# Strassen's seven products in place of eight for two projection banks of the first eight token tiles

## The chip, the cores and the metric

The kernel runs on one core of a Trainium2 chip. The metric is the device time of one execution in microseconds (us), the median of several runs. The engines are named as in the profile: PE is the matrix engine (TensorE), PEld its weight load, DVE the vector engine, ACT the scalar engine, POOL the GpSimd engine, and SP the engine whose queue issues the DMA transfers. A "bank" is one of the eight PSUM banks, 128 rows by 512 float32 columns.

## The reference, cut to what matters

The block adds to its input x (2048 tokens of 640 features) a linear attention over the normalised x and an MLP over the twice normalised x.

```python
xn = _layernorm(x)
q, k, v = split(xn @ wqkv)                   # 32 heads of 20
pq, pk = q @ w_phi, k @ w_phi                # per head
phi = concat([softmax(p), softmax(-p)])      # for pq and for pk
kv, z = phi_k^T @ v, sum(phi_k)              # per head
o = (phi_q @ kv) / (phi_q @ z + 1e-6)
out = x + o @ wo + gelu(layernorm(xn) @ w1 + b1) @ w2 + b2
```

Softmax over 20 features needs a maximum, a minimum, two differences, an exponential and a sum for k and for q of each token.

## The kernel before, in words

All large products are done in float32 exactly split into two parts, "hi" and "lo" (`split`: ACT writes hi as a rounded copy, DVE or POOL writes lo as the difference). A product of two split matrices takes three matmuls: hi by hi, hi by lo, lo by hi.

The work stands in stages that follow each other on PE. First come the MLP passes of the first 1024 tokens (`Mlp.passes(g, b, ...)`, g from 0 to 6 for hidden chunks and b 0 or 1 for 512 tokens each); beside them the other engines prepare: `prep` folds w_phi into wk and wq (tiles wkh and wkl, 128 rows by 5 chunks of the contraction by their columns) and writes the normalised tokens 1024 to 2047 to DRAM. From there to about 430 us stand the projections of 16 token tiles of 128 tokens. The rest of the span holds the MLP of the second 1024 tokens, the attention and the output projection. In the MLP of the second half and in the output projection the kernel before already uses Strassen's scheme.

A projection tile t has four banks, in the order i = 0, 1, 2, 3: columns 0 to 511 (features of k), 512 to 1023 (the rest of k, then features of q), 320 columns (the rest of q, a part of v), and 512 columns of v. `proj(t, i)` issues the 15 matmuls of one bank, 5 chunks by 3, into one of three rotating banks (`ptile`, banks 0 to 2). `evacuate` copies a bank with ACT into one of four buffers `pks` (two in tile m3, two in m4): 0 for k, 1 + t % 3 for q. `features` takes maximum and minimum on DVE (L932, L933), two differences on POOL (L938), the exponential on ACT (L939) and the sum on DVE (L941), in one of three buffers e (m0, m1, m2 in turn). `k_tile` divides on POOL (L949) and splits the result into the one buffer ft (tile w1, L60 and L63); `q_tile` divides on POOL (L992, L995) and transposes on DVE (L1001). `v_parts` splits v out of the bank (ACT L965, DVE L967). `kv_tile(t - 2)` multiplies ft by v into the five banks 3 to 7 (L974), and once into a rotating bank (L978) that DVE adds to kxa. The split of wo (L60, L63, five of them) stands beside tiles 1, 2, 3, 6 and 7.

On PE everything is in the order in which it is written. DVE, ACT and POOL are in written order up to the end of the MLP passes (`order.close()`) and again late in the span; in the projections a list scheduler sets their order when the program is built, so that each of these engines has one fixed queue. A tile with one buffer is given out again when its last reader is done.

Of the kernel before, what the change touches and what calls it, by code (L numbers as in the profile page):

```python
# [15 lines left out]
P = 128  # L16
# [34 lines left out]
def tile_kernel(ctx: ExitStack, tc: tile.TileContext, x, xT, wkT, wqT, wv, wphi, wo, w1, b1, w2, b2,  # L51
# [42 lines left out]
    a_dram = [tc.dram_tile([P, KC, 512], F32, name=f"a{b}") for b in range(2)]  # L94
    d_dram = [[tc.dram_tile([H, 512], F32, name=f"d{i}{b}") for i in range(2)] for b in range(NB)]
# [555 lines left out]

    jobs = [units[o:o + 2] for o in range(0, 14, 2)]
# [54 lines left out]
    wkv_ = [kvw.tile([P, KC, CN], F32R, name=f"wk{p}") for p in "hl"]  # L707
    def prep_fold(batch, ts, done=None):
# [26 lines left out]
    def more_stats():  # L735

        def tiles():
            xbs = {}
            for t in (*range(8, 16), None):
                if t is not None:  # L740
                    xbs[t] = fp.tile([P, 2, KC, G5], F32, name="t").rearrange("p a c f -> p (a c f)")[:, :D]
# [4 lines left out]
        yield from stats(range(8, 16), fp, tiles())  # L746
        for _ in range(2):
            yield
        yield from rows(2, 2, fp, mlp.px, 5)

    def prep():
# [18 lines left out]
        split(*[w[:, :, C2:C3] for w in wkv_], raw)  # L770

        xs, hls, events = {}, {}, []

        def load(c, b):
            xs[c, b] = fp.tile([P, 512], F32, name="xq", bufs=4)
# [9 lines left out]
        def hi(*at):  # L785
            hls[at] = fp.tile([P, 2, KC, G5], F32R, name="t").rearrange("p a c f -> p a (c f)")[:, :, :512]
# [23 lines left out]

        base = 8
# [18 lines left out]

    def load_v():

        raws = [fp.tile([P, 2, KC, G5], F32, name="t").rearrange("p a c f -> p (a c f)") for _ in range(2)]
        raws = [raw[:, o:o + VF * H] for raw in raws for o in (0, VF * H)] + [fp.tile([P, D], F32, name="raw")[:, :VF * H]]
# [9 lines left out]

    p01 = mlp.passes(0, 1, [wc[0], wc[1]])
    next(p01)
    mlp.beside = prep()
# [9 lines left out]
    for g in range(2, 7):  # L857
        for b in range(2):
# [4 lines left out]
            if (g, b) == (6, 1):  # L863
                mlp.beside = split_v()
# [13 lines left out]
    rs.close()  # L878
    order.close()
    for b in range(2):  # L880
# [6 lines left out]
    acc[2] = ctx.enter_context(tc.tile_pool(name="acc2", bufs=1)).tile([P, KC, 512], F32, name="acc2")  # L887
# [14 lines left out]
    def proj(t, i):  # L902
# [4 lines left out]
        ps = ptile()[:, :wh.shape[2]]  # L907
# [19 lines left out]
    def features(t, n):  # L927

        turn[0] += 1
        p3 = pks[0 if n == "k" else 1 + t % 3].rearrange("p (h f) -> p h f", f=DH)  # L930
# [13 lines left out]
    def k_tile(t):  # L944
        e, sm = features(t, "k")
# [6 lines left out]
        split(fh, fl, e)  # L952
# [17 lines left out]
    def kv_tile(t, ft, v):  # L970
# [6 lines left out]
        ps = ptile()[:, :160]  # L977
# [7 lines left out]
    def q_tile(t):  # L985


        e, sm = features(t, "q")
# [9 lines left out]
        if i == 0:  # L998
            ets[b] = [places[n % 5] for n in range(4 * b, 4 * b + 4)]
# [9 lines left out]
    fts, ets = {}, {}  # L1009
    TAIL = [(14, 0), (14, 1), (15, 0), (15, 1), (14, 2), (14, 3), (15, 2), (15, 3)]  # L1010
    places = [acc01.tile([P, KC, 512], F32, name=f"acc{n}").rearrange("p c (j n) -> p (c j) n", n=P) for n in range(2)]
    places = [p[:, j:j + 10] for p in places for j in (0, 10)] + [et.tile([P, 10, P], F32, name="et")]


    for t, i in [(t, i) for t in range(14) for i in range(4)] + TAIL:
        if (t, i) in ((4, 0), (8, 0)):
            b = t // 4 + 1
            y[b] = [yp.tile([P, KC, 512], F32R, name=f"y{p}{b % 2}") for p in range(2)]
            for p in range(2):
                nc.sync.dma_start(f(y[b][p]), y_dram[b - 2][p])  # L1020
        ps = proj(t, i)
        pq = 1 + t % 3
        if t and t % 4 == 0:
# [7 lines left out]
        elif i == 2:  # L1031
            evacuate(ps[:, C3 - C2:], pq, B1F)
            v_parts(t, ps, VF)
            q_tile(t)
# [636 lines left out]
```

## Time and profile before

| what | value |
|---|---|
| median of 3 runs | 700.89 us (700.73 to 700.99) |
| the profiled execution | 701.24 us |
| its span | 699.5 us |
| PE busy | 693.6 us, 99% of the span |
| DVE, ACT, POOL busy | 523.3, 365.2, 437.9 us |
| projections of 16 tiles | from about 211 to 430 us |
| granted clock of PE | 1.0 |

The span is the time from the first to the last recorded instruction; the rest of the execution lies around it. Busy time of an engine is the union of its instructions. A group of instructions is given with its count, its busy time and the mean time of one; for PE that mean is the latency of one matmul, and the time from one start to the next is shorter, since matmuls overlap.

### The profile page before, as it was taken

How to read it: one execution, taken by the hardware profiler on the slowest of the kernel's cores; microseconds unless marked ns; L12 is line 12 of the kernel's file. 1: busy time of each engine (PE TensorE's matmuls, PEld its weight loads, DVE VectorE, ACT ScalarE, POOL GpSimd, SP SyncE). 2: the span in 40 equal slices, each digit the busy share in tenths (PEclk: the TensorE clock that was granted, in tenths of full speed). 3: DMA queues.
4: the chain of work that ended last, by engine and by line, in shares of the span. 5: the costliest groups of instructions: out<-in, count | busy, mean ns of one | idle time of the engine just before them, and what ended most of it. 6: DMA issues, size and time to landing. Idle time of an engine off the chain costs nothing.

```text
span 699.5 us, 9720 instructions
## 1 busy us (share of the span) xinstructions
PE 693.6 (99%) x3331; PEld 584.8 (84%) x3331; DVE 523.3 (75%) x859; ACT 365.2 (52%) x617; POOL 437.9 (63%) x324
## 2 busy tenths in 40 slices
PE   8999999999999999999999999999999999999998
PEld 7888888888888888888888888888888888888886
DVE  7778654987754787788878888948688686789783
ACT  6434643344433545554544546557676666659350
POOL 3711314566245886687666869648689997577930
PEclk9999999999999999999999999999999999999999
DMA  9834633485634227326500705874355548881222
GB/s 315 256 126 124 198 109 99 158 268 172 210 116 155 81 90 227 93 75 205 136 1 1 189 0 201 284 210 128 111 149 160 184 148 291 287 278 63 76 76 105
DMA packets 67463, 107.61 MB, mean 154 GB/s; under 512 B 7622, under 2 KB 31974, under 8 KB 65790
## 3 DMA queue, kind: packets, MB, share of 16 engines
q1 hardware_dynamic: 67110, 106.98, 48.1%
q8 instruction: 26, 0.43, 0.3%
q14 instruction: 23, 0.19, 0.1%
q10 hardware_dynamic: 304, 0.01, 0.0%
HBM read 72.42 MB, written 34.55 MB: 153 GB/s over the span
## 4 chain that ended last, share of the span: by engine, by line
PE 96%; DVE 2%; DMA 0%; issue 0%; ACT 0%; DVEq 0%
PE bank L913 29%; PE bank L69 19%; PE bank L70 19%; PE bank L71 19%; PE bank L974 3%; PE bank L648 2%; PE bank L1208 1%; PE bank L1209 1%; PE bank L554 1%; PE bank L313 1%; PE bank L332 1%; PE bank L312 1%; PE bank L331 1%; DVE st L137 0%; DMA xb<-in_x 0%; DVE rx L1257 0%
## 5 line engine op out<-in xcount | busy, mean ns | idle before, releaser
L913 PE MATMUL bank<-wkh,y 128*128 128x512 f32 (+1 forms) x480 | 139.8, 365 | 0.0
L69 PE MATMUL bank<-m,w 128*128 128x512 f32 x288 | 113.1, 393 | 0.0
L70 PE MATMUL bank<-m,w 128*128 128x512 f32 x288 | 112.2, 390 | 0.0
L63 POOL TENSOR_TENSOR w<-r,w 128x640 fp32r<-128x640 f32 x32 | 52.6, 1656 | 92.8 <-ACT w L60 62.3
L71 PE MATMUL bank<-m,w 128*128 128x512 f32 x266 | 103.7, 390 | 0.0
L69 PE MATMUL bank<-y,w 128*128 128x512 f32 (+1 forms) x256 | 99.7, 389 | 0.0
L70 PE MATMUL bank<-y,w 128*128 128x512 f32 (+1 forms) x256 | 99.0, 387 | 0.0
L913 PEld LDWEIGHTS bank<-wkh,y 128*128 128x128 f32 x480 | 87.5, 188 | 12.9
L71 PE MATMUL bank<-y,w 128*128 128x512 f32 (+1 forms) x246 | 95.1, 387 | 0.0
L913 PE MATMUL bank<-wkl,y 128*128 128x512 f32 (+1 forms) x240 | 87.1, 363 | 0.0
L69 PEld LDWEIGHTS bank<-m,w 128*128 128x128 f32 x288 | 54.1, 188 | 11.4 <-issue 0.4
L70 PEld LDWEIGHTS bank<-m,w 128*128 128x128 f32 x288 | 54.1, 188 | 10.9
L938 POOL TENSOR_TENSOR m<-m,mx 128x640 f32<-128x640 f32 x32 | 42.1, 1315 | 31.9 <-DVE mx L932 31.8
L939 ACT ACTIVATE m<-m,rs_all 128x1280 f32<-128x1280 f32 x32 | 43.7, 1364 | 30.4 <-POOL m L938 30.4
L71 PEld LDWEIGHTS bank<-m,w 128*128 128x128 f32 x266 | 49.9, 188 | 10.4
L941 DVE TENSOR_REDUCE sm<-m 128x64 f32<-128x1280 f32 x32 | 47.3, 1477 | 13.9 <-ACT m L939 13.7
L336 DVE TENSOR_TENSOR acc<-bank,acc 128x512 f32<-128x512 f32 x70 | 47.3, 684 | 13.6 <-PE bank L71 8.4
L913 PE MATMUL bank<-w,y 128*128 128x512 f32 x240 | 57.4, 391 | 0.0
L69 PEld LDWEIGHTS bank<-y,w 128*128 128x128 f32 x256 | 48.1, 188 | 10.4 <-ACT bank L1276 0.3
L70 PEld LDWEIGHTS bank<-y,w 128*128 128x128 f32 x256 | 48.1, 188 | 9.4
L71 PEld LDWEIGHTS bank<-y,w 128*128 128x128 f32 x246 | 46.2, 188 | 9.4
L949 POOL TENSOR_TENSOR m<-m,w 128x1280 f32<-128x1280 f32 x16 | 39.2, 2448 | 20.4 <-DVE w L947 18.4
(242 smaller groups left out, 1524.7 us busy)
## 6 DMA issues: line engine op xcount, KB each, us to landing
r<-in_w SPq DMA_DIRECT2D x52, 320.0 KB
e<-e SPq DMA_DIRECT2D x40, 256.0 KB
e<-acc SPq DMA_DIRECT2D x52, 160.0 KB
t<-t SPq DMA_DIRECT2D x8, 512.0 KB
acc<-in_xT SPq DMA_DIRECT2D x3, 1280.0 KB
tf<-t SPq DMA_DIRECT2D x2, 1536.0 KB
xb<-in_x SPq DMA_DIRECT2D x8, 320.0 KB
t<-in_x SPq DMA_DIRECT2D x8, 320.0 KB
```

The lines of the kernel that those rows point to most:

```text
L63: eng.tensor_tensor(lo, src, f(hi), op=ALU.subtract)
L69: nc.tensor.matmul(ps, lh, rh, start=first, stop=False, **kw)
L70: nc.tensor.matmul(ps, lh, rl, start=False, stop=False, **kw)
L71: nc.tensor.matmul(ps, ll, rh, start=False, stop=last, **kw)
L336: nc.vector.tensor_tensor(acc[b][:, m, :], pw, acc[b][:, m, :], op=ALU.add)
L648: nc.tensor.matmul(ps[:, u * nh * DF:(u + 1) * nh * DF], raw[:nh * DH, u * P:(u + 1) * P], wpt[:nh * DH, g, :nh, 1:], start=True, stop=True)
L913: nc.tensor.matmul(ps, lh[:, kc, c], rh[:, kc], start=n == 0, stop=n == 3 * KC - 1)
L938: subs[n, t] = nc.gpsimd.tensor_tensor(ep[:, :, s], a, b, op=ALU.subtract)
L939: exps[n, t] = nc.scalar.activation(e, e, AF.Exp, scale=rs_all[:, t:t + 1])
L941: nc.vector.tensor_reduce(sm, e.rearrange("p a (h f) -> p (a h) f", f=DH), axis=AX, op=ALU.add)
L949: nc.gpsimd.tensor_tensor(e3, e3, w.unsqueeze(2).to_broadcast([P, 2 * H, DH]), op=ALU.mult)
L974: nc.tensor.matmul(kvp[g // 2][:, (g % 2) * 240:(g % 2) * 240 + 240].rearrange("p (i c) -> p i c", i=2), v[:, g * VS:(g + 1) * VS], ft[:, ...
```

## The change

For tokens 0 to 1023 the tiles are taken in pairs, (0, 1) to (6, 7), and banks 0 and 1 of a pair are computed together. Of the five contraction chunks, 0 and 1, and 2 and 3, form two 2x2 block products (token tile by chunk, times chunk by bank). Each takes seven block products in Strassen's form (Winograd's variant) in place of eight; chunk 4 (`rest`) is done as before.

- On the side of the weights four sums of blocks, s1 to s4, are needed for each pair of chunks q. `raw_sums` builds them (four adds on DVE, four on POOL for each q), `split_sums` splits them (ACT and DVE). For q = 0 the raw sums stand in the events of `prep`, their splits in `sums_end` beside the last two MLP passes (g = 6), where the raw sums for q = 1 stand too; the splits for q = 1 follow the MLP (`late`). s3 replaces the block a21 in wkh and wkl, which is stored to DRAM before (`open_sums`) and loaded back after the last pair.
- On the side of the tokens four differences t1 to t4 are built on POOL beside the MLP passes (`turned_forms`: for each of two 512-token blocks and each q, 2 adds of 512 columns and 4 subtractions of 256), split on ACT and DVE and stored to DRAM in 16 transfers; `load_forms` loads 1 MB of them before each pair into the one buffer w0.
- On PE a pair has 7 x 2 x 3 + 4 x 3 = 54 matmuls for the two banks, where the two tiles had 2 x 2 x 15 = 60. `sevens` sets their order: bank 0 holds product a11 b11, to which s2 t2 and then s3 t3 and a rest are added, and each time a partial sum is complete it is copied out (ACT) before PE goes on in that bank; bank 1 holds s1 t1, to which s4 b22 is added; bank 2 holds two products that are only added. So of the four results of a pair each is an ACT copy (`move`, L1174) and then a DVE add (L1172) into `pks`.
- `pks` 0 and 1 are now k of the two tiles, 2 and 3 their q. The lo part of k features is half on DVE and half on POOL. PE's order in the first pair is: bank i = 2 of both tiles (`narrow`), i = 3 of both (`wide`), then `sevens`; the next pair's `sevens` follow at once. In later pairs: `sevens` (with `kv_tile(t - 2)` in it), two `narrow`, `wide(0, 2)`, `kv_tile(t - 1)`, `wide(1, 2)`; both `wide` use bank 2.
- The splits of wo stand beside tiles 8, 9 and 10.

Tiles 8 to 15 are computed as before. The core of the diff:

```diff
-    def proj(t, i):
+    def proj(t, i, ps=None):
...
-        ps = ptile()[:, :wh.shape[2]]
+        ps = (ps or ptile())[:, :wh.shape[2]]
...
-        p3 = pks[0 if n == "k" else 1 + t % 3].rearrange("p (h f) -> p h f", f=DH)
+        p3 = pks[i].rearrange("p (h f) -> p h f", f=DH)
...
-        split(fh, fl, e)
+        if t < 8:
+            nc.scalar.activation(fh, e, AF.Copy)
+            for s, eng in enumerate((nc.vector, nc.gpsimd)):
+                eng.tensor_tensor(fl[:, s], e[:, s], f(fh[:, s]), op=ALU.subtract)
+        else:
+            split(fh, fl, e)
...
+    def pair(t, yt, start):
...
+        def product(ps, w, yn, first=False, last=False):
+            for q in range(2):
+                for n, (pl, pr) in enumerate(((0, 0), (0, 1), (1, 0))):
+                    nc.tensor.matmul(ps, left(yn, pl, q), right(w, pr, q), start=first and q == 0 and n == 0,
...
+        def move(ps, i, j, add):
+
+            parts = [(ps, j, 1)] if i == 0 else [(ps[:, :KQ - 512], j, 1 + 512 // H), (ps[:, KQ - 512:], 2 + j, 1)]
...
+                if add:
+                    nc.vector.tensor_tensor(o, src, o, op=ALU.add)
+                else:
+                    nc.scalar.activation(o, src, AF.Copy)
...
+        def sevens():
+            a = bank(0)
+            product(a, "a11", "b11", True)
+            move(a, 0, 0, False)
+            z = bank(1)
+            product(z, "s1", "t1", True)
+            move(z, 1, 1, False)
+            c = bank(2)
+            product(c, "a12", "b21", True)
+            rest(c, 0, 0)
+            move(c, 0, 0, True)
+            product(a, "s2", "t2")
+            move(a, 0, 1, False)
+            product(z, "s4", "b22")
+            rest(z, 0, 1)
+            move(z, 0, 1, True)
+            product(a, "s3", "t3")
+            move(a, 1, 0, False)
+            c = bank(2)
+            product(c, "a22", "t4", True)
+            rest(c, 1, 0)
+            move(c, 1, 0, True)
+            fts[t] = k_tile(t, 0)
+            kv(0, 1)
+            rest(a, 1, 1)
+            move(a, 1, 1, True)
+            fts[t + 1] = k_tile(t + 1, 1)
...
+        if start:
+            for j, i in ((0, 1), (1, 0)):
+                v_parts(ts[j], narrow(j, i), VF)
+            for j, i in ((0, 2), (1, 1)):
+                wide(j, i)
+            sevens()
+            for j in range(2):
+                q_tile(ts[j], 2 + j)
+            return
...
+        sevens()
...
+        v_parts(ts[0], narrow(0, 1), VF)
+        q_tile(ts[0], 2)
+        ps = narrow(1, 0)
+        q_tile(ts[1], 3)
+        wide(0, 2)
+        kv(1, 1)
+        v_parts(ts[1], ps, VF)
+        wide(1, 2)
```

Three places show how the queues now stand. The first is POOL's queue at the first tiles. Names: m3 and m4 hold `pks`, mx the maximum and minimum, m0 to m2 the buffers e, w1 the buffer ft, sm and w the sums and their reciprocals. Before, k and q of tile 0 and then k of tile 1:

```order
L938 TENSOR_TENSOR m1_2089<-m3_2043,mx_2086 128x32x20
L938 TENSOR_TENSOR m1_2089<-mx_2086,m3_2043 128x32x20
L938 TENSOR_TENSOR m2_2124<-m3_2043,mx_2121 128x32x20
L938 TENSOR_TENSOR m2_2124<-mx_2121,m3_2043 128x32x20
L949 TENSOR_TENSOR m1_2089<-m1_2089,w_2095 128x1280
L63 TENSOR_TENSOR r1_2175<-r1_2175,r2_2176 128x640
L992 TENSOR_TENSOR w_2130<-sm_2128,w_2130 128x32
L995 TENSOR_TENSOR m2_2124<-m2_2124,w_2130 128x32x20
L938 TENSOR_TENSOR m0_2202<-m3_2043,mx_2199 128x32x20
```

In the changed kernel, k of tiles 0 and 1 (m3) and q of tile 0 (m4), and, behind the division and split of k, q of tile 1 (m1_2381):

```order
L1040 TENSOR_TENSOR m1_2327<-m3_2170,mx_2324 128x32x20
L1040 TENSOR_TENSOR m1_2327<-mx_2324,m3_2170 128x32x20
L1040 TENSOR_TENSOR m2_2348<-m3_2170,mx_2345 128x32x20
L1040 TENSOR_TENSOR m2_2348<-mx_2345,m3_2170 128x32x20
L1040 TENSOR_TENSOR m0_2364<-m4_2171,mx_2361 128x32x20
L1040 TENSOR_TENSOR m0_2364<-mx_2361,m4_2171 128x32x20
L1051 TENSOR_TENSOR m1_2327<-m1_2327,w_2333 128x1280
L1057 TENSOR_TENSOR w1_2336<-m1_2327,w1_2336 128x640
L1051 TENSOR_TENSOR m2_2348<-m2_2348,w_2354 128x1280
L1099 TENSOR_TENSOR w_2370<-sm_2368,w_2370 128x32
L1040 TENSOR_TENSOR m1_2381<-m4_2171,mx_2378 128x32x20
L1040 TENSOR_TENSOR m1_2381<-mx_2378,m4_2171 128x32x20
```

The four features of a pair now come together, and the fourth stands last, since its buffer e (m1) is the one that k of tile 0 held until its split.

The second place is DVE's queue around the read of v (L967 before, L1074 now, 480 and 32 columns) in tile 2. Before:

```order
L967 SCALAR_TENSOR_TENSOR v0_2037<-bank2_2341,rs_all_64,v0_2037 128x11x12
L941 TENSOR_REDUCE sm_2332<-m2_2328 128x64
L967 SCALAR_TENSOR_TENSOR v0_2037<-bank0_2377,rs_all_64,v0_2037 128x10x48
L967 SCALAR_TENSOR_TENSOR v0_2037<-bank0_2377,rs_all_64,v0_2037 128x32
L947 RECIPROCAL w_2334<-sm_2332 128x64
L941 TENSOR_REDUCE sm_2367<-m0_2363 128x64
```

Now, with two sums and a reciprocal ahead of it, and the bank (bank2) the one that PE takes for the next `wide`:

```order
L1043 TENSOR_REDUCE sm_2469<-m2_2465 128x64
L1034 TENSOR_REDUCE mx_2565<-m4_2171 128x32
L1035 TENSOR_REDUCE mx_2565<-m4_2171 128x32
L1049 RECIPROCAL w_2471<-sm_2469 128x64
L1043 TENSOR_REDUCE sm_2503<-m0_2499 128x64
L1074 SCALAR_TENSOR_TENSOR v0_2164<-bank2_2582,rs_all_64,v0_2164 128x10x48
L1074 SCALAR_TENSOR_TENSOR v0_2164<-bank2_2582,rs_all_64,v0_2164 128x32
L1090 TENSOR_TENSOR kxa_2163<-bank1_2602,kxa_2163 123x160
```

Before, the bank that DVE read (bank0) came back to PE three projections later; now bank2 comes back after the eleven matmuls of `kv_tile`.

The third place is DVE's queue at the end of the MLP (g = 6), where each L336 (before) or L338 (now) adds a finished bank 5, 6 or 7 to acc. Before:

```order
L336 TENSOR_TENSOR acc0_103<-bank5_1934,acc0_103 128x512
L336 TENSOR_TENSOR acc0_103<-bank6_1943,acc0_103 128x512
L336 TENSOR_TENSOR acc0_103<-bank7_1952,acc0_103 128x512
L919 MEMSET m4_2044 128x32 x2
L336 TENSOR_TENSOR acc0_103<-bank5_1961,acc0_103 128x512
L336 TENSOR_TENSOR acc0_103<-bank6_1970,acc0_103 128x512
```

Now, with the raw sums (L871) and the lo parts (L884) of the weights between:

```order
L338 TENSOR_TENSOR acc0_106<-bank5_2031,acc0_106 128x512
L871 TENSOR_TENSOR xq_2041<-wkh_593,wkl_594 128x512
L338 TENSOR_TENSOR acc0_106<-bank6_2048,acc0_106 128x512
L1021 MEMSET m4_2171 128x32 x2
L884 TENSOR_TENSOR wkl_594<-acc2_1300,wkh_593 128x512
L871 TENSOR_TENSOR xq_2042<-wkh_593,wkl_594 128x512
L338 TENSOR_TENSOR acc0_106<-bank7_2059,acc0_106 128x512
L338 TENSOR_TENSOR acc0_106<-bank5_2070,acc0_106 128x512
L1021 MEMSET m3_2170 128x32 x2
L884 TENSOR_TENSOR m5_2039<-acc2_1300,m5_2039 128x512
L871 TENSOR_TENSOR xq_2043<-wkh_593,wkl_594 128x512
```

Eight instructions now stand among the ten adds that free PE's banks.

More of the change, by code (lines that the diff above doesn't have):

```diff
@@ L650, in products, with both, late_start @@
         return us, ps
+    def both(*gens):
+        for _ in zip_longest(*gens):
+            yield
+    def late_start(n, gen):
+        for _ in range(n):
+            yield
+        yield from gen
     jobs = [units[o:o + 2] for o in range(0, 14, 2)]
@@ L829, in prep, with open_sums @@
             step(*args)
+    temps, spare, forms = [], [], {}
+    def open_sums():
+        own["a"] = ctx.enter_context(tc.tile_pool(name="acc2", bufs=1))
+        own["s"] = ctx.enter_context(tc.tile_pool(name="s12", bufs=1))
+        t = own["a"].tile([P, KC, 512], F32, name="acc2")
+        temps.extend(t[:, i] for i in range(4))
+        spare.append(t[:, 4])
+        for q in range(2):
+            for p in range(2):
+                nc.sync.dma_start(s_dram[:, q, p], f(wkv_[p][:, 2 * q, 512:1024]))
@@ L877, in tile_kernel @@
     finish(mlp.beside)
-    rs.close()
     order.close()
+    for step in late:
+        step()
+    gs.close()
     for b in range(2):
@@ L998, in q_tile @@
         if i == 0:
[L999 removed]
+            ets[b] = [turns[n % 5] for n in range(4 * b, 4 * b + 4)]
         for n, et in enumerate(ets[b]):
@@ L1051, in tile_kernel @@
         if (t, i) == (9, 0):
+            acc[2] = own["a"].tile([P, KC, 512], F32, name="acc2")
             load_acc(2)
```

182 lines of the change are left out of this document (148 added, 34 removed).

## The prediction

> **What bounds the kernel now.** I read the page first: which engine is busy, and which chain ends last.
>
> ```profile
> span 699.5 us, 9720 instructions
> PE 693.6 (99%) x3331; PEld 584.8 (84%) x3331; DVE 523.3 (75%) x859; ACT 365.2 (52%) x617; POOL 437.9 (63%) x324
> PE 96%; DVE 2%; DMA 0%; issue 0%; ACT 0%; DVEq 0%
> ```
>
> PE works 99% of the span and is 96% of the chain that ended last. So a matmul taken away is worth its full time, and a wait put on PE costs its full time, wherever it stands. Next the chain in order of time in the projections (start, us, what):
>
> ```profile
> 240.57 12.52 PE bank L913 x60
> 253.09 1.13 PE bank L974 x10
> 254.29 12.52 PE bank L913 x60
> ...
> 405.21 10.29 PE bank L913 x45
> ```
>
> The last row is 45 matmuls of 512 columns: 10.29 / 45 = 0.229 us each. A whole tile (45 of 512 and 15 of 320 columns) takes 12.52 us, so one of 320 columns takes (12.52 - 10.29) / 15 = 0.149 us; kv takes 1.13 us and one more short matmul. PE goes from tile to tile without a gap, 13.72 us each. The windows tell what the other engines have left beside it (us; PE, PEld, DVE, ACT, POOL busy, clock, DMA share, GB/s); the second is a tile without a split of wo:
>
> ```profile
> 60.00:110.00 50.00, 50.00 (x261) 42.65 (x260) 33.63 (x83) 25.13 (x50) 12.40 (x8) 1.00 0.49 147
> 280.50:294.20 13.70, 13.70 (x73) 11.87 (x72) 11.41 (x18) 5.56 (x10) 8.93 (x7) 1.00 0.36 82
> ```
>
> In a projection tile DVE is busy 11.4 of 13.7 us: PE waits for nobody only because three banks rotate and nothing that PE needs soon hangs on a feature. The change alters just that, so I need the durations in this stage. Groups by line, 211 to 349 us, POOL, DVE and ACT:
>
> ```profile
> L938 POOL TENSOR_TENSOR m<-m,mx 128x640 f32<-128x640 f32 x20 | 26.8, 1339 | 17.0 <-DVE mx L932 16.8
> L938 POOL TENSOR_TENSOR m<-mx,m 128x640 f32<-128x640 f32 x20 | 25.6, 1278 | 2.1 <-DVE mx L933 2.1
> L949 POOL TENSOR_TENSOR m<-m,w 128x1280 f32<-128x1280 f32 x9 | 21.3, 2370 | 14.3 <-DVE w L947 12.3 <-ACT m L925 2.0
> L995 POOL TENSOR_TENSOR m<-m,w 128x640 f32<-128x640 f32 x9 | 11.5, 1276 | 0.7
> L63 POOL TENSOR_TENSOR r<-r,r 128x640 fp32r<-128x640 f32 x5 | 7.9, 1578 | 1.9 <-ACT r L60 1.9
> ...
> L941 DVE TENSOR_REDUCE sm<-m 128x64 f32<-128x1280 f32 x19 | 28.0, 1472 | 6.1 <-ACT m L939 6.1
> L932 DVE TENSOR_REDUCE mx<-m 128x32 f32<-128x640 f32 x20 | 15.9, 796 | 7.7 <-ACT m L925 7.7
> L63 DVE TENSOR_TENSOR w<-m,w 128x1280 fp32r<-128x1280 f32 x9 | 14.3, 1586 | 14.0 <-ACT w L60 13.9
> L967 DVE SCALAR_TENSOR_TENSOR v<-bank,rs_all,v 128x480 fp32r<-128x480 f32 x10 | 7.1, 711 | 2.2 <-ACT v L965 2.1
> L967 DVE SCALAR_TENSOR_TENSOR v<-bank,rs_all,v 128x32 fp32r<-128x32 f32 x10 | 2.4, 242 | 0.0
> L983 DVE TENSOR_TENSOR kxa<-bank,kxa 123x160 f32<-123x160 f32 x7 | 2.2, 321 | 1.4 <-PE bank L978 1.4
> L336 DVE TENSOR_TENSOR acc<-bank,acc 128x512 f32<-128x512 f32 x1 | 0.7, 691 | 0.4 <-PE bank L332 0.4
> ...
> L939 ACT ACTIVATE m<-m,rs_all 128x1280 f32<-128x1280 f32 x20 | 27.3, 1366 | 18.2 <-POOL m L938 18.2
> L60 ACT ACTIVATE w<-m 128x1280 fp32r<-128x1280 f32 x9 | 11.5, 1276 | 13.4 <-POOL m L949 13.4
> L965 ACT ACTIVATE v<-bank,rs_all 128x480 fp32r<-128x480 f32 x10 | 6.6, 659 | 8.6 <-PE bank L913 8.5
> L925 ACT ACTIVATE m<-bank 128x416 f32<-128x416 f32 x10 | 5.2, 521 | 0.0
> L965 ACT ACTIVATE v<-bank,rs_all 128x32 fp32r<-128x32 f32 x10 | 2.7, 274 | 0.0
> ```
>
> **The change, part by part.** Sums are made against the profiled execution, 701.24 us (span 699.5 and 1.7 around it); the median of the runs is 0.35 lower.
>
> 1. *Matmuls removed.* 60 - 54 = 6 of 512 columns a pair, four pairs: 24 x 0.229 = -5.5 us. All on PE's path. Weight loads go with them.
>
> 2. *The first pair into the second.* In bank 1 PE may add s4 b22 only when ACT has copied s1 t1 out, and that copy writes `pks` 1 and 3. Buffer 3 holds q of the tile before, free only when POOL has taken both differences of it. In the first pair all four features begin at its very end. I count from the end of PE's last product in bank 2 of that pair. DVE adds 512 columns in two pieces: a PSUM add into a strided place is not in the trace; L336 (0.69 us) is nearest, and 0.8 for two pieces. Then the maximum, 0.80. POOL starts at about 1.7 and has, in its order: six differences 6 x 1.28 = 7.7; the division of k 2.37; a wait for ACT's hi 1.28 (L60); its half of lo, 1.58 (a full 640 columns of two inputs, like r<-r,r); the next division 2.37; a short one, 0.26 (next fence); two differences 2.56. That is 18.1, so 19.8. On ACT the exponential of that tile stands ahead of the copy: 1.37 and 0.52. Less some 0.4 for the overlap of successive starts: PE can go on at 21.3 us. Until then it has 3 + 6 + 6 + 9 + 6 = 30 matmuls, 6.9 us. So PE stands idle 14.4 us, some 2.4 of it before the next pair's first product: its bank 0 waits for an add that DVE has behind a maximum and a minimum. Bounds: 12 (ACT copies ahead of the exponential, handoffs short) and 17. The load of the second pair's t forms (1 MB) starts when the first pair's are read; even in a stage with the DMA engines half busy, 147 GB/s, it takes 1.05 / 0.147 = 7 us beside that, within the 14.4: nothing.
>
> 3. *Both wide banks in bank 2.* In pairs 2 to 4, `wide(1, 2)` comes 11 short matmuls (1.2 us) after `wide(0, 2)`, and needs ACT's and DVE's read of it: 0.66 + 0.27 and 0.71 + 0.24, with handoffs 1.9. So 0.7 us even if both stood free. DVE has the sum of another feature (1.47) ahead: 2.2. An exponential on ACT (1.37) may add to it: 3.3. I take 2.2, since that order is fixed: 3 x 2.2 = 6.6, bounds 2.1 and 9.9. Queued behind the waiting matmul is all of PE's later work, so the next pair starts that much later.
>
> 4. *The end of the MLP.* DVE gets four raw sums and four lo parts among ten adds to acc. The rows for two SBUF inputs, 512 columns, 160 to 211 us:
>
> ```profile
> L808 DVE TENSOR_TENSOR t<-xq,t 128x512 fp32r<-128x512 f32 x4 | 5.5, 1384 | 1.7 <-ACT t L787 1.7
> ...
> L791 DVE TENSOR_TENSOR t<-xq,t 128x512 fp32r<-128x512 f32 x4 | 3.3, 815 | 0.1
> ```
>
> and one POOL row of the projections by its minimum, median and maximum:
>
> ```profile
> L992 POOL TENSOR_TENSOR w<-sm,w x9: 252/260/1512, 230.2 to 338.0; 128x32 f32<-128x32 f32 x9
> ```
>
> The raw sums run while POOL works, so 1.38; the lo parts 0.82: 8.8 us. With ten adds of 0.69 DVE has 15.7 us where PE has 10 x 5 x 0.229 = 11.4. Two banks in hand hide 2.3: 2.0 us of waiting (0 to 3.5; the floor if DVE's idle time there takes more).
>
> By the Trainium skill, "SBUF — State Buffer", section "SBUF: two separate sides", a DVE instruction with two SBUF inputs and a POOL instruction hold one port pair by turns, for a whole instruction. The rows above agree: the same shape takes 0.82 or 1.38 us, and a POOL instruction of 0.26 once took 1.51. By it DVE's half of lo (0.8, half of L63) would go ahead of POOL's in part 2: 0.8 us more, and the whole sum 0.8 higher.
>
> 5. *kv beside the seven products.* Its last matmul goes to bank 1, which `narrow` needs three matmuls (0.7) later. kxa (0.32) stands on DVE behind a maximum and a minimum (1.6): 1.2 us, in the pair where these have just begun. Bounds 0 and 3.6 (three pairs); I take one.
>
> 6. *PE's clock after the long wait.* No row shows PE idle for long inside the span. The nearest is its start (start, us; 18 equal matmuls of 512 columns):
>
> ```profile
> 1.31 5.83 PE L582 MATMUL bank<-m 128*128 128x512 f32 x18 [1.31 <-POOL m L580]
> ```
>
> 18 x 0.229 and the 0.16 by which the last one's latency exceeds its step make 4.3; they took 5.83: 1.5 us lost at the start. After 12 us of nothing I take the same, 1.5; floor 0.
>
> 7. *The later pairs' own copy into buffer 3.* From kv(t - 1): hi 1.28, lo 1.58, division 2.37, two differences 2.56, exponential 1.37, copy 0.52, handoffs 0.5 = 10.2. PE has 15 + 27 matmuls (9.6) and the 2.2 of part 3, 11.8. Hidden, unless the first division (2.37) is late, for which POOL has reason: 0.8 each, two boundaries, 1.6. Bounds 0 and 6.
>
> 8. *wo beside tiles 8 to 10, and what the pairs leave behind.* Five splits (1.58 POOL each) in 34 us, where they were in five tiles, and DVE and POOL come to tile 8 late: 0 to 5, I take 2.5.
>
> 9. *At nothing:* POOL's building of t beside the MLP (by 1.58 for 640 columns, 8 x 1.3 and 16 x 0.7 = 22 us) and raw sums: POOL is busy 12.4 of 50 us there. If that cover fails, DVE's lo waits for POOL and PE's banks for DVE, some tenths. The 4 MB stored and the reload of a21: DMA share 0.49 there and 0.36 in the tile shown. ACT has 5.56 of 13.7.
>
> Sum: -5.5 + 14.4 + 6.6 + 2.0 + 1.2 + 1.5 + 1.6 + 2.5 = +24.3. 701.24 + 24.3 - 0.35 = 725.2; I say 725.5. Less than 0.2%, 1.4 us, could not be told from no change here.
>
> **The rivals.**
>
> - *Only the first boundary costs.* For it: DVE has 2.3 us of 13.7 to spare, and the list scheduler's queue may still serve v in time. Against it: even free engines leave 0.7 in part 3. Without parts 3, 5, 7, 8: 725.5 - 11.9 = 713.6.
> - *DVE and POOL become the bound of the pairs.* Per pair DVE has 2 x 11.4, four adds of 0.7, less one lo of 1.6: 24.0 of PE's 54 x 0.229 + 30 x 0.149 + 30 x 0.229 + 2.4 = 26.1. If each of some five two-input instructions is stretched by 0.6 as in L808, and by 0.8 on POOL, a pair takes 29: three times 3 on top, 734.
> - *Faster, by the matmuls alone.* It decides where the chain of part 2 ends: PE has 6.9 us of work, so it must end within 6.9 + 5.5 - 2.1 (part 3's floor) = 10.3 in place of 21.3; POOL's part alone is 18.1, by rows of 9 and 20 instructions with means of 1.28 and 2.37. Then 700.9 - 5.5 + 2.1 = 697.5.
> - *No change:* waits that happen to eat the 5.5; 701.
>
> **How the numbers follow.** My forecast, 0.62, own range 719 to 732; only the first boundary 0.15; DVE and POOL as the bound 0.17; faster 0.04; no change 0.02. So slower by over 0.2% 0.94, within it 0.02, faster 0.04. Range 713 to 737: from the second case to beyond the third; all floors together would give 709.5 (-5.5 + 12 + 2.1), all ceilings 742 (-5.5 + 17 + 9.9 + 3.5 + 3.6 + 1.5 + 6 + 5).
>
> **What would show it.** PE's 512-column matmuls 24 fewer (right by the code; their step should stay 0.229). Part 2: in PE's waits one of 12 us before a product in bank 1, released by ACT's copy, POOL busy nearly throughout before it; part 6: matmuls at double step after it. Part 3: three waits of some 2 us at 512-column v banks, released by DVE. Part 4: PE waiting for adds to acc at the MLP's end. Wrong, if PE stays at 99% of the span, or if the waits stand in the MLP stage, where I put almost nothing.

## The result, and the profile after

The changed kernel took 743.85 us (median of 4 runs, 742.31 to 747.85), the kernel before beside it 700.94 (700.73 to 701.98): a ratio of 1.0618, with a 95% interval of 1.0573 to 1.0662. It is 43 us slower; forecast were 24 us, and the range ended at 737. The profiled execution took 743.01 us, its span 741.0, 41.5 us more than before. From its page:

```profile
span 741.0 us, 9857 instructions
PE 700.8 (95%) x3307; PEld 584.7 (79%) x3307; DVE 559.0 (75%) x907; ACT 373.8 (50%) x633; POOL 483.7 (65%) x364
PE   9999999999989658988999999999999999999998
PEclk9999999999999969999999999999999999999999
PE 65%; DVE 15%; POOL 7%; DMA 5%; issue 4%; ACT 3%; SPq 0%; POOLq 0%; ACTq 0%; DVEq 0%
```

The 24 matmuls are gone (3331 before, 3307 now), yet PE is busy 7 us longer, mainly because some of its matmuls ran at half clock: the slice with the 6 in the clock row. PE's share of the chain that ended last fell from 96% to 65%; the rest stands with DVE, POOL and others that PE waited for. Who these are, from PE's waits (us in total, times, longest):

```profile
PE bank L1154 <- ACT m L1174: 13.6, 3, 12.6
PE bank L1015 <- DVE v L1074: 8.4, 6, 2.7
PE bank L69 <- DVE acc L338: 4.5, 5, 2.9
PE bank L1154 <- DVE m L1172: 2.4, 1, 2.4
PE bank L650 <- issue: 1.5, 1, 1.5
...
PE bank L1015 <- DVE kxa L1088: 0.7, 1, 0.7
```

Row 1 holds the first pair's boundary (12.6), row 2 the second wide group of pairs 2 to 4 in bank 2 (7.3 of the 8.4; the rest stands behind the pairs), row 3 the end of the MLP, row 4 the wait ahead of the second pair's first product, row 5 the fold of w_phi, where the forecast had nothing. The clock follows in windows (us; PE, PEld, DVE, ACT, POOL busy, granted clock, DMA share, GB/s); each pair of rows is a stretch with a wait in it and the one behind it:

```profile
210.20:213.61 3.41, 0.64 (x3) 0.58 (x4) 3.41 (x7) 1.74 (x4) 3.41 (x3) 1.00 0.00 0
213.61:217.03 3.42, 3.42 (x9) 2.11 (x7) 3.42 (x3) 0.00 (x0) 3.42 (x3) 0.50 0.03 5
254.58:257.99 3.41, 0.36 (x2) 0.00 (x0) 3.41 (x5) 2.73 (x3) 2.38 (x2) 1.00 0.00 0
257.99:271.64 13.65, 4.14 (x10) 3.31 (x11) 4.71 (x9) 2.19 (x3) 9.51 (x8) 0.50 0.00 0
285.30:288.71 3.41, 1.79 (x14) 1.55 (x12) 3.41 (x5) 3.31 (x5) 3.32 (x3) 1.00 0.00 0
288.71:292.12 3.41, 2.28 (x10) 1.94 (x11) 3.41 (x8) 1.58 (x2) 2.02 (x2) 1.00 0.00 0
316.02:319.43 3.41, 1.16 (x10) 1.03 (x10) 3.41 (x8) 3.11 (x5) 3.31 (x3) 1.00 1.01 234
319.43:322.84 3.41, 3.41 (x9) 2.66 (x9) 3.41 (x5) 1.69 (x2) 2.03 (x2) 0.50 0.15 30
346.74:350.15 3.41, 1.16 (x12) 1.03 (x10) 3.41 (x8) 3.11 (x5) 3.31 (x4) 1.00 0.00 0
350.15:353.56 3.41, 3.41 (x8) 2.68 (x9) 3.41 (x5) 1.81 (x2) 2.03 (x2) 0.50 0.00 0
```

Four stretches at 0.50, where the forecast had one. A stretch of 3.41 us in which PE is busy costs half of itself, 1.7; in the long one PE was busy 4.14, so 2.07 are lost there: 3 x 1.7 + 2.07 = 7.2 us.

To find where the 41.5 us arose I compared the start of the same matmul in both traces. The lag is 3.8 us at the end of the fold (103 us of the changed kernel), 4.5 by 170 us, 10.6 at the end of the MLP (220 us), 37.2 behind the eight paired tiles, 41.4 at 433 us and 41.5 at the end. So the preparation lost 10.6, the pairs 26.6 although they do 5.5 less, tiles 8 to 10 lost 4.3.

### The profile page after: what moved, and what is told of

Read it like the earlier page. It is cut to its first block, busy times and chain, and to the rows that moved or that the text cites. A ratio compares the mean times of both kernels' runs of the same rounds, so it can differ in the third digit from the quotient of the medians.

```text
span 741.0 us, 9857 instructions
## 1 busy us (share of the span) xinstructions
PE 700.8 (95%) x3307; PEld 584.7 (79%) x3307; DVE 559.0 (75%) x907; ACT 373.8 (50%) x633; POOL 483.7 (65%) x364
## 4 chain that ended last, share of the span: by engine, by line
PE 65%; DVE 15%; POOL 7%; DMA 5%; issue 4%; ACT 3%; SPq 0%; POOLq 0%; ACTq 0%; DVEq 0%
PE bank L69 15%; PE bank L71 15%; PE bank L70 15%; PE bank L1015 9%; POOL m L1040 4%; PE bank L1154 3%; POOL m L1051 2%; DVE acc L338 2%; DMA r<-in_wo 2%; DMA wol<-r 1%; PE bank L1445 1%; PE bank L1446 1%; PE bank L650 1%; DVE mx L1035 1%; DVE sm L1043 1%
## 5 line engine op out<-in xcount | busy, mean ns | idle before, releaser
L1015 PE MATMUL bank<-wkh,y 128*128 128x320 f32 (+1 forms) x320 | 88.9, 352 | 3.1 <-ACT m L1027 1.2
L69 PEld LDWEIGHTS bank<-m,w 128*128 128x128 f32 x288 | 54.2, 188 | 18.3 <-DVE acc L338 3.9
L1015 PE MATMUL bank<-w,y 128*128 128x512 f32 x240 | 60.7, 407 | 7.3 <-DVE v L1074 7.3
L1015 PEld LDWEIGHTS bank<-wkh,y 128*128 128x128 f32 x320 | 57.3, 188 | 11.2 <-ACT m L1027 2.0
L1015 PEld LDWEIGHTS bank<-w,y 128*128 128x128 f32 x240 | 46.7, 198 | 17.1 <-issue 7.6
L71 PEld LDWEIGHTS bank<-m,w 128*128 128x128 f32 x266 | 50.1, 188 | 10.6
L1015 PE MATMUL bank<-wkl,y 128*128 128x320 f32 (+1 forms) x160 | 55.9, 349 | 0.0
L338 DVE TENSOR_TENSOR acc<-bank,acc 128x512 f32<-128x512 f32 x70 | 46.7, 681 | 6.5 <-PE bank L71 4.8
```

What stands on the lines that cost most here:

```text
L69: nc.tensor.matmul(ps, lh, rh, start=first, stop=False, **kw)
L71: nc.tensor.matmul(ps, ll, rh, start=False, stop=last, **kw)
L338: nc.vector.tensor_tensor(acc[b][:, m, :], pw, acc[b][:, m, :], op=ALU.add)
L1015: nc.tensor.matmul(ps, lh[:, kc, c], rh[:, kc], start=n == 0, stop=n == 3 * KC - 1)
```

## The experiments

**Preparation or pairs?** The old loop beside the new preparation; restored columns first, tiles 0 to 7 bank by bank:

```diff
-    for t in range(0, 8, 2):
-        pair(t, yt, t == 0)
...
+    FIRST = [(0, 3), (1, 3), (0, 0), (0, 1), (0, 2), (1, 0), (1, 1), (1, 2)]
+    for t, i in FIRST + [(t, i) for t in range(2, 14) for i in range(4)] + TAIL:
```

> The changed kernel's preparation (the sums and split parts of t, their 16 stores, the raw sums and split parts of s) with the first eight tiles projected bank by bank as in the kernel before, with its order, its wo splits, and k's low parts on one engine; the third of wkv that s overwrote is loaded back at once and the two wide groups of tiles 0 and 1 stand first, over that load. Theory (most of the loss is in the pairs): the preparation's own price stays, 4.5 us by 165 us and 6.1 us in the MLP's last 20 us, and 0 to 3 us for the reload: 711 to 714. Rival (the preparation is the main cost, its stores and port use going on under the first tiles): 725 or more.

Measured: 713.38 us (713.05 to 713.62), ratio 1.0178 (1.0162 to 1.0193). The lag behind the kernel before is 4.4 by 103 us, 11.1 at the MLP's end, 12.1 by 253 us, 12.3 by 266 us and no more after that; one stretch of half clock, at the MLP's end. The theory's figure. So the preparation, with the reload of the restored columns, costs 12.5 us by itself, and the pairs with the moved wo splits 30.5.

**What of the preparation?** First t; without it the pairs load other numbers in its place:

```diff
-    mlp.beside = both(prep(), late_start(18, turned_forms()))
+    mlp.beside = prep()
```

> The changed kernel without the work on t: its sums, differences, split parts and stores are left out, and the pairs load y's chunks in their place (so the outputs are other numbers). GpSimd loses 24 instructions and some 22 us of work between 37 and 104 us, VectorE and ScalarE 8 each, SyncE 16 stores. Theory (shared work in the fold stage): the 3.8 us lost between 81 and 102 us and the rest of the 4.5 us by 165 us come back: 739 to 740. Rival (the other pool of the stage and its fewer buffers make the loss): 743 as before.

Measured: 739.26 us (738.68 to 740.29), 4.6 less, 4.1 of it won by 99 us. The fold's stretch in three kernels, before, changed, and without t:

```profile
75.00:105.00 30.00, 30.00 (x157) 25.60 (x156) 17.79 (x49) 17.09 (x37) 6.23 (x5) 1.00 0.45 130
```

```profile
75.00:105.00 30.00, 27.15 (x142) 22.93 (x141) 27.15 (x56) 17.75 (x39) 25.96 (x23) 1.00 0.73 215
```

```profile
75.00:105.00 30.00, 30.00 (x157) 25.50 (x156) 17.82 (x49) 17.45 (x38) 6.21 (x4) 1.00 0.41 122
```

PE is busy the whole time where t is not built. With t, POOL works 26 of 30 us instead of 6, and DVE 27 instead of 18. Most of DVE's 9.4 us are t's low parts (groups by line and shape of the changed kernel, 75 to 105 us):

```profile
L906 DVE TENSOR_TENSOR m<-xq,m 128x512 fp32r<-128x512 f32 x6 | 8.1, 1349 | 0.0
```

1.35 us each, beside a busy POOL. An edit meant to move the stores alone:

```diff
-                        nc.sync.dma_start(f_dram[b][:, :, q, i, p]...
+                        held.append(lambda ...: nc.sync.dma_start(f_dram[b][:, :, q, i, p]...
```

> The changed kernel, with the 16 stores of t's split parts (f, 256 KB each) issued a few steps later, when the parts they store are done, so that the queue of SyncE does not stand before them with the raw loads of the fold behind it. Theory (queue order): the waits of the fold's products near 83 and 94 us (1.15 and 1.56 us) and most of the 3.8 us that the changed kernel loses between 81 and 102 us go: 3 to 4 us shorter, 739 to 741. Rival (shared work): the loss there is GpSimd's and VectorE's added instructions delaying the planner's steps; then the time stays within 1 us of 743.

Measured: 742.79 us (741.96 to 743.94). The fold's waits stayed (1.6 and 1.0 us), 1.1 us less is within the spread of the changed kernel's own runs. But the edit did not move the stores: in its trace SyncE's queue has its 423 transfers in the same order as in the changed kernel, and each of the 16 stores goes out 0.1 to 0.3 us later. So the order of that queue was not tested and stays a possible cause: in the changed kernel two stores (75.49 and 76.82 us) stand ahead of a load of the fold that goes out at 77.29 us, where it went out at 75.58 before and at 75.35 without t. Whether DVE's and POOL's work, the traffic of the stores or their place in the queue takes the 4 us is not separated: leaving t out takes away all three.

**The pairs: which buffer, which bank?** A fourth buffer for q of tile 1:

```diff
-        e = mtile(turn[0] % 3)
+        e = mtile(turn[0] % 3) if (n, t) != ("q", 1) else turns[4]...
```

> The changed kernel, with a buffer of its own for the exponentials of tile 1's q (it uses the tile et, which is not written before tile 4). Theory (buffer): TensorE's wait of 12.6 us at s4 x b22 of the second pair comes from GpSimd doing tile 0's product with w and low part before it can take the differences for q of tile 1, and ScalarE's exp for q(1) standing ahead of the move that frees bank 0. With the buffer the two differences follow the six others (the last one would end near 257.1 us, exp 1.4, move 0.5): the wait shrinks to 4 to 5 us, the half-clock stretch there from 13.65 us to one of 3.41, and the kernel is about 8 us shorter, 734 to 737. Rival (GpSimd's throughput): GpSimd is simply behind by 10 us of work at this place, what is taken out of this wait comes back as a wait for the low part of k of tile 0 at the first kv product, and the time stays within 2 us of 743.

Measured: 739.91 us (737.79 to 742.97). At the place the theory is right: POOL does the last difference at 257.91, PE goes on at 261.03 after 3.98 us.

```profile
256.68 1.27 POOL L1040 TENSOR_TENSOR et<-m,mx 128x640 f32<-128x640 f32 x1
257.91 1.27 POOL L1040 TENSOR_TENSOR et<-mx,m 128x640 f32<-128x640 f32 x1
...
260.48 0.50 ACT L1174 ACTIVATE m<-bank 128x416 f32<-128x416 f32 x1
...
261.03 1.22 PE L1154 MATMUL bank<-r,y 128*128 128x512 f32 x2 [3.98 <-ACT m L1174]
```

Of the 8.5 us won there 5.4 were lost again by 350 us: a wait for kxa rose from 0.7 to 2.2, and half-clock stretches stand at 259 (6.83 us long, where the theory had 3.41), 273, 287 and 317 us. Another one behind the fold (95 us) has nothing to do with the edit. So the cause of this wait was found and its price was not: neither sum is right. Then the wide groups:

```diff
-        wide(0, 2)
-        kv(1, 1)
-        v_parts(ts[1], ps, VF)
+        kv(1, 2)
+        v_parts(ts[1], ps, VF)
+        wide(0, 1)
         wide(1, 2)
```

> The changed kernel, with the end of pairs 2 to 4 in another order: kv of the second tile into bank 2, then wide of the first tile into bank 1, then wide of the second into bank 2, so that the two wide groups no longer follow each other through bank 2. Theory (one bank): the three waits for the low part of v (2.76, 2.27 and 2.27 us, 7.3 in sum) go, and with them the two half-clock stretches behind them (3.41 us each, some 1.7 us lost in each): about 10 us shorter, 732 to 735. Rival (DVE's queue): the low part is late because VectorE is behind, so the wait moves to the next pair's use of banks 1 and 2 with 1.5 to 2.5 us each, and the time falls by 3 us at most.

Measured: 750.20 us (749.17 to 750.29), 6.4 slower than the changed kernel, which neither side expected. In the pairs the waits of the wide groups are gone (the v waits ahead of projections fell from 8.4 to 2.6 us, and what is left is one wait at 395 us), a wait of 1.9 us for v came up ahead of the third pair's next product in bank 2, as the rival has it, and the waits for ACT's copy rose from 13.6 to 18.1 (11.2, 2.4 and 4.6). The boundary of the third pair:

```profile
294.08 2.95 POOL L1051 TENSOR_TENSOR m<-m,w 128x1280 f32<-128x1280 f32 x1
...
297.21 1.27 POOL L1040 TENSOR_TENSOR m<-m,mx 128x640 f32<-128x640 f32 x1
298.44 1.27 POOL L1040 TENSOR_TENSOR m<-mx,m 128x640 f32<-128x640 f32 x1
...
302.81 0.51 ACT L1174 ACTIVATE m<-bank 128x416 f32<-128x416 f32 x1
...
303.38 1.22 PE L1154 MATMUL bank<-r,y 128*128 128x512 f32 x2 [2.36 <-ACT m L1174]
```

It is the first boundary's chain again: q of the odd tile (the differences at 297 us) stands behind k's division, since it has to take over k's buffer. In the changed kernel the wide waits had covered it. And PE, with other waits, had seven half-clock stretches instead of four: three times 1.7 is 5 of the 6.4 us, by that estimate. Both edits together, with the buffer in every pair:

```diff
+    def own_e(t):
+        return turns[4 - t // 4]...
...
+        e = own_e(t) if n == "q" and t < 8 and t % 2 else mtile(turn[0] % 3)
```

> The changed kernel with the wide order of the run e_wide_order and a fourth buffer for the exponentials of q of every odd one of the first eight tiles (turns[4] for tiles 1 and 3, turns[3] for 5 and 7, both free at that time). In e_wide_order the waits on the low part of v fell from 8.4 to 2.6 us and two new waits of some 3.5 us came up at s4 x b22 of the third and fourth pair, for a move into the copy that q's differences of the odd tile still read. Theory (the same held buffer in every pair): with it both kinds of wait are gone, together 8.6 us at the first boundary, 7.3 us of wide waits and about 3.4 us of half clock: 722 to 727. Rival (GpSimd and VectorE as the bound of the pairs, 21 and 24 us of work in each 30 us but in one long chain): the waits come back elsewhere, as waits for k's low part or for copies, and the time stays above 735.

Measured: 732.21 us (731.08 to 734.23), 11.6 less. The waits for ACT's copy are down to 2.4 us, those for v to 2.5; waits for kxa (4.0 in all) and for the add into `pks` (2.4) are left, and half-clock stretches of together 20.5 us. Between the two expectations: the buffer was the cause in every pair, but of the 17.1 us of waits taken away (11.2 and 5.9) only 11.6 were won.

**Is it PE's idleness that halves its clock?** 48 needless matmuls in the long wait:

```diff
+            if t == 2:
+                for _ in range(48):
+                    nc.tensor.matmul(kvp[0], y[b][0][:, 0, cs[0]], wkv_[0][:, 1, 0:512], start=True, stop=True, ...)
             product(z, "s4", "b22")
```

> The changed kernel with 48 more products of 128x512 (into bank 3, which kv starts afresh afterwards), placed where TensorE waits 12.6 us in the second pair: 48 x 0.2275 = 10.9 us of work that no result needs. Theory (clock): what halves TensorE's clock is its own idleness, so with the wait filled the half-clock stretch of 13.65 us at 257 us is gone and the products behind the wait run at 0.23 us instead of 0.42: some 2 us shorter there (released at 267 us as before, at 271.5 us two us ahead of the changed kernel), although TensorE does 10.9 us more work. Rival (the clock follows something else, such as the load of the whole core): the stretch stays and the time is the same or, where the 48 products end late, longer by up to 2 us.

Measured: 740.10 us (739.43 to 744.02). The same stretch of time as the fourth row of windows above, now at full clock:

```profile
257.99:271.64 13.65, 13.46 (x60) 10.79 (x59) 5.47 (x11) 2.50 (x4) 8.76 (x8) 1.00 0.00 0
```

The first product behind the wait starts 0.2 us later than in the changed kernel, the one 38 matmuls on 2.3 us earlier. PE did 10.9 us more work and the products behind the wait came earlier: for this wait it is shown that PE's idleness halves the clock. The kernel's median is 3.7 us lower, in ranges that overlap.

**The end of the MLP, and wo.**

```diff
         ops = raw_sums(1, ts)
+        late.extend(ops)
+        ops = ()
```

> The changed kernel, with the sums of wkv's second pair of chunks (VectorE, 128x512 each) issued behind the MLP instead of among its last additions. Theory (stretched sums): the two-input sums of 1.7 us each stand ahead of the last acc additions; without them there the waits of 3.04, 0.85 and 0.53 us at 212 to 220 us and the half-clock stretch at 213 us (1.7 us lost) go: 5 to 6 us shorter at that place. Rival (only moved): the sums have to be done before the s and t products of the first pair, which begin about 10 us later, and VectorE's work of 8 sums and 8 splits then ends too late: a wait of 3 to 8 us at the first pair's s1 x t1 or s2 x t2, and the time within 2 us of 743 or above it.

Measured: 746.69 us (746.33 to 748.14). At the MLP's end the theory's mechanism holds: longest wait 1.3 instead of 2.9, no half clock, 3.3 us won, where it had 5 to 6. The s and t products did not wait longer, against the rival. But 2.1 us had been lost by 99 us, ahead of the edit, with a half-clock stretch in the fold, and from 386 us on 4.9 and then 2.6 us more, at a place that neither named (3.8 of these came back by 433 us, where the changed kernel has waits of its own):

```profile
388.70 0.74 ACT L60 ACTIVATE r<-r 128x640 fp32r<-128x640 f32 x1 [5.93 <-DMA r<-in_wo]
389.35 0.82 ACT L1074 ACTIVATE v<-bank,rs_all 128x480 fp32r<-128x480 f32 x2
...
391.23 0.77 PE L1017 MATMUL bank<-wkh,y 128*128 128x512 f32 x1 [4.42 <-DVE v L1076]
```

ACT's copy of wo waits 5.93 us for its load, v's copy stands behind it, and PE's bank behind that. So:

```diff
-    SPLITS = [(8, 1), (8, 3), (9, 1), (9, 3), (10, 1)]
+    SPLITS = [(8, 1), (9, 1), (10, 1), (11, 1), (12, 1)]
```

> The changed kernel with the five wo splits one per tile ((8,1), (9,1), (10,1), (11,1), (12,1)) instead of one in every second group from (8,1) to (10,1). Theory (load in ScalarE's queue): each split's load waits for the stores of the one before it, and ScalarE's copy of it waits 7.1 us in all for the loads with the bank copies behind it; with a tile between them the loads are there in time, as in the kernel before, and the waits of TensorE near 405 and 417 us (1.4, 0.8 and 0.7 us) and most of the 4.3 us lost from tile 8 on go: 740 to 742. Rival (backlog of the last pair's features): the copies are late because k and q of tiles 6 to 8 crowd on GpSimd, and the time stays within 1 us of 743.8.

Measured: 745.89 us (744.93 to 746.96). From 386 to 433 us this kernel loses nothing more on the kernel before, where the changed kernel loses 4.3; it comes out 3.1 ahead of it there, as the theory has it, and 5.8 are lost between 433 and 470 us, where the last splits now stand: a wait of 3.5 us for v, with a half-clock stretch. The mechanism at tiles 8 to 10 is right, the new place is as bad. The wide order, the own buffers, the sparse splits and a later start of k's features together; the last is new:

```diff
-            fts[t] = k_tile(t, 0)
             kv(0, 1)
             rest(a, 1, 1)
             move(a, 1, 1, True)
+            fts[t] = k_tile(t, 0)
```

> The run e_own_buffer_all_wide (732.2 us) with the wo splits one per tile and with the features of a pair's first k tile started behind the last move of the pair's banks, so that VectorE does that move (waited for 2.4 us at 248 us) ahead of the reductions. Theory (each is a wait of its own): 1.5 us at the first boundary and 2 to 3 us after tile 8 less: 727 to 729. Rival (what is taken from one wait comes back in the next, as kv's wait for k's low part): 731 or more. Neither expects it under 701: the preparation alone made 713.4, and the products removed are worth 5.5.

Measured: 732.08 us (731.42 to 733.50), nothing won on 732.21, the rival's figure. The wait of 2.4 us for the add is still there, but DVE's queue at that place is also what it was (the last row is the add that PE waits for):

```profile
249.00 0.81 DVE L1037 TENSOR_REDUCE mx<-m 128x32 f32<-128x640 f32 x1
249.73 0.81 DVE L1038 TENSOR_REDUCE mx<-m 128x32 f32<-128x640 f32 x1
250.46 0.75 DVE L1175 TENSOR_TENSOR m<-bank,m 128x96 f32<-128x96 f32 x2
```

The maximum and the minimum still stand ahead of the add, so the edit did not change the order that it was to change, and whether that order is worth the 1.5 us that the two take is not tested.

With the edit of e_sums_after_mlp on top of these:

```diff
+        late.extend(ops)
+        ops = ()
```

> The run e_combined with the second raw sums issued behind the MLP as in e_sums_after_mlp. There 3.3 us were won at the MLP's end and more than that lost again from 386 us on, where a copy of wo stood in ScalarE's queue 5.9 us before its load had landed. Theory (that loss was wo's load, no price of the moved sums): with the sparse splits the win stays, 2.5 to 4 us under e_combined. Rival (the moved sums delay the s parts and with them the first pairs): no gain, or a loss of up to 2 us.

Measured: 726.36 us (725.13 to 727.77), 5.7 under e_combined; the theory's direction and more than its figure. Its trace has half-clock stretches of 10.2 us in all, that of e_combined 20.5, one of them in the fold, ahead of the edit. The first half-clock stretch of this kernel stands at 246.9 us.

**Half clock after a wait of 2.4 us.** Two fillers, of 8 and 16 matmuls, in that kernel:

```diff
+            if t == 2:
+                for _ in range(8):
+                    nc.tensor.matmul(kvp[0], ...)
             product(a, "a11", "b11", True)
...
+            if t == 2:
+                for _ in range(16):
+                    nc.tensor.matmul(kvp[0], ...)
             product(z, "s4", "b22")
```

> The run e_combined_sums (726.4 us) with 8 more products of 128x512 (1.8 us) where TensorE waits 2.4 us ahead of the second pair's first product and 16 (3.6 us) where it waits 2.4 us ahead of s4 x b22, all into bank 3, which no result needs then. Theory (a stretch of 3.41 us in which TensorE idles more than about 1.9 us is followed by one at half clock): the half-clock stretches at 246 and 256 us go, the one behind the 2.7 us wait at 268 us stays; the first win only lengthens the second wait, whose end GpSimd sets, so 1.7 us are won by 262 us, and 0 to 1.7 of them are left at the end: 724.5 to 726.5. Rival (waits of 2.4 us and the clock are unrelated at this size, or the products added stand in the way): both stretches stay, or the time is above 727.

Measured: 724.06 us (723.26 to 724.38), a little under the theory's range. Without the fillers:

```profile
243.47:246.88 3.41, 1.41 (x6) 1.24 (x7) 3.41 (x7) 0.26 (x1) 2.80 (x3) 1.00 0.62 262
246.88:250.29 3.41, 3.41 (x9) 2.65 (x8) 3.41 (x5) 2.83 (x3) 3.41 (x4) 0.50 0.00 0
253.71:257.12 3.41, 1.27 (x6) 1.06 (x7) 3.31 (x4) 2.86 (x4) 3.41 (x3) 1.00 0.00 0
257.12:260.53 3.41, 3.41 (x10) 2.64 (x9) 3.00 (x5) 0.50 (x1) 3.41 (x3) 0.50 0.00 0
```

With them:

```profile
243.47:246.88 3.41, 2.78 (x13) 2.02 (x12) 3.41 (x7) 0.17 (x1) 2.71 (x3) 1.00 0.68 279
246.88:250.29 3.41, 3.41 (x17) 2.83 (x16) 3.41 (x4) 2.82 (x3) 3.41 (x3) 1.00 0.00 0
253.71:257.12 3.41, 3.02 (x14) 2.18 (x13) 3.29 (x4) 2.44 (x3) 3.41 (x3) 1.00 0.00 0
257.12:260.53 3.41, 3.41 (x17) 2.82 (x16) 2.69 (x4) 1.27 (x3) 3.41 (x3) 1.00 0.00 0
```

Both stretches run at 1.00 now; the third, at 267 us, went too, which was not expected (its wait fell from 2.7 to 2.2 us), and one came up at 426 us, behind a wait of 2.1 us that had cost no clock without the fillers. This is the best version, and it still takes 1.0332 (1.0315 to 1.0349) of the time before. None of the runs points to a version that beats the kernel before: the preparation costs 12.5 us as the change has it, the matmuls saved are worth 5.5.

## Why the prediction was wrong, and where it was right

| part | forecast | in the changed kernel's trace |
|---|---|---|
| 1 matmuls removed | -5.5 | -5.5: 24 fewer |
| 2 first boundary | 14.4 | 15.0: waits of 2.4 and 12.6 |
| 3 wide in bank 2 | 6.6 | 7.3: 2.7, 2.3 and 2.3 |
| 4 end of the MLP | 2.0 | 4.5 |
| 5 kv and kxa | 1.2 | 0.7 |
| 6 clock | 1.5, once | 7.2, at four places |
| 7 later copies into buffer 3 | 1.6 | 1.0: 13.6 less 12.6 |
| 8 tiles 8 to 10 | 2.5 | 4.3 |
| 9 t and its stores | 0 | 4.5 |

The column sums to 39.0 of the 41.5 us. The 2.5 left have no part of their own; 0.5 is a wait before a product of the first pair (235 us), and an estimate covers the rest: the 13 waits of parts 2 to 5 and 7 each cost some 0.16 more than their length, the time by which a matmul's latency (0.39) exceeds its step (0.23).

*Right:* the direction, and parts 1, 2, 3, 5 and 7: 18.3 forecast, 18.5 measured. The chain of part 2 is shown by e4_own_buffer, which cut the wait by 8.6 with nothing but a buffer. In the changed kernel POOL's half of lo took 2.18 us beside DVE's, where the sum had 1.58: most of the 0.8 that the prediction named and left out. What part 7 called its cover, the wait of part 3, was the cover: e_wide_order took it away and the hidden chain came up.

*Wrong, part 6,* the largest: one loss of 1.5, taken from the span's start, for "12 us of nothing". Behind the long wait 2.1 were lost, near that figure; the other 5.1 stand behind short waits, which halve the clock as well (e_combined_filled), so parts 3 and 4 each brought a price in clock that I had not put on them.

*Wrong, part 9:* costed at nothing because POOL was busy 12.4 of 50 us. The part named what would fail ("DVE's lo waits for POOL and PE's banks for DVE") but priced it at some tenths. In the 30 us where it fell, POOL went to 26, and the run without t won 4.6 us. Which of t's work, traffic and stores in the queue makes the price stays open.

*Wrong, part 4:* the size of two rows. Raw sums were taken at 1.38 and low parts at 0.82; DVE's groups of the changed kernel, 200 to 222 us, show

```profile
L871 DVE TENSOR_TENSOR xq<-wkh,wkl 128x512 f32<-128x512 f32 x4 | 5.3, 1338 | 0.0
...
L884 DVE TENSOR_TENSOR m<-acc,m 128x512 fp32r<-128x512 f32 x2 | 3.5, 1764 | 0.0
```

the sums as forecast, the low parts at twice their figure, for POOL was busy beside them too. With 1.7 for the four low parts the part's own working gives 2.0 + 4 x 0.88 = 5.5.

*Wrong, part 8,* within its bounds of 0 to 5: the splits' POOL time was counted; what cost was the load in front of them in ACT's queue (ACT waits 7.1 us for it in the changed kernel, from 376 to 440 us). The chain stands in the rows of e_sums_after_mlp, and e_wo_sparse did not lose the 4.3 us there, though its edit also thins out the splits on POOL.

The rival with DVE and POOL as the bound has something for it: much of the waits taken away in the pairs came back as others. But its 734 came from three other microseconds per pair, and its sum had the same gaps in parts 4, 6 and 9. The range was too narrow at the top, because it stopped short of its own ceilings (742) and held the clock at 1.5 in all of them.

## What to carry to other kernels

Where the matrix engine is busy 99% of the span, count a new wait with what it does to the clock, not only with its length, and look in the trace for how long a wait must be for that. A wait's length is the price of its place, not of its cause: taking away 8.6 us won 3.9, and taking away a wait that covered another one lost 6.4. Cover for moved work is to be read in the 20 or 30 us in which it falls, by the engine and its neighbour, not from a mean over the stage. And an edit of an order is a test only if the trace shows the order changed: two of these left the queue as it was.

## What the runs showed of the hardware

**PE's clock.** From 20 us on, all stretches at half clock inside the spans of the changed kernel and the twelve runs last 3.41 us or a multiple of it, on a grid that goes on through each run. I laid each trace's grid over its matmuls, from 20 to 460 us, with a matmul's end taken 0.16 us before the recorded one: of the full-clock stretches with at least 0.9 us idle in them, 53 were followed by half clock, with 1.84 to 3.41 us idle, and 72 were not, with 0.92 to 1.98. So the cut lies at 1.8 to 2.0 us of 3.41. With the recorded ends, as in the windows above, it is less sharp: 1.52 to 3.41 against 0.92 to 1.87. A wait of 2.3 us costs 1.7 more if it falls into one stretch (316 us in the windows above) and nothing if the grid cuts it (the wait of 2.7 at 285 to 292 us, 1.62 and 1.13 idle). That may be why the changed kernel's runs lie 5.5 us apart and the former's 1.3: the two shorter ones have a mean granted clock of 0.984, the two longer ones 0.976. It was not tested. By the Trainium skill, "TensorE: Matmul & The Clock Gate", section "Part 1: The HAM clock gate", the gate goes to half rate after at least one idle window, a free-running one of 3413 ns: the grid agrees, but not the whole window has to be idle, 54 to 58% are enough here by the first count, and by its rule only the long wait would have cost clock.

**DVE beside POOL.** The same DVE sum of two SBUF inputs took 0.67 us with POOL idle at 206 us and 1.75 at 210 us beside POOL's splits, while adds with one PSUM input (L338) stayed at 0.68:

```profile
206.36 0.67 DVE L871 TENSOR_TENSOR xq<-wkh,wkl 128x512 f32<-128x512 f32 x1
210.47 1.75 DVE L871 TENSOR_TENSOR xq<-wkh,wkl 128x512 f32<-128x512 f32 x1
```

The Trainium skill, "SBUF — State Buffer", section "SBUF: two separate sides", has POOL and a DVE instruction with two SBUF inputs lock one shared port pair by turns, for whole instructions; the trace agrees, with a price of 0.5 to 1.1 us for each such instruction beside a busy POOL (1.16 to 1.76 us in place of 0.67).
